# GpSimd takes the last state of a scan unit, its sums stand behind that state, ScalarE's scan copies move behind a product's copy, and the last stores use two queues

## The chip, the cores and the metric

The kernel runs on one core of a Trainium2 chip. The metric is the device time of one execution in microseconds (us); the kernel before is given by the median of three timed runs. A profile of one more execution shows what each engine did: PE (TensorE, the matrix unit; its weight loads are listed as PEld), DVE (VectorE), ACT (ScalarE), POOL (GpSimd) and SP (SyncE, which issues most DMAs). A sequencer's own work is marked with a q behind the engine (SPq, ACTq).

## The reference

Two computations follow each other. The first is a state-space scan (Mamba-2) over 4 batches, 8 heads and 768 time steps with head dimension 32 and state dimension 16:

```python
state = 0
for each chunk c of the sequence:
    cum = cumsum(log(clip(a, 1e-6, 1)))               # within the chunk
    L   = exp(cum[i] - cum[j]) for i >= j, else 0
    y[chunk]  = ((C B^T) * L) x  +  (C state) * exp(cum)
    state     = exp(sum(la)) * state + sum_j exp(cum[-1] - cum[j]) B_j x_j
```

Its output, rearranged to 3072 tokens by 256, goes through a feed-forward block:

```python
h = x @ w_in            # 256 -> 2048
g = h / (1 + exp(-h))   # silu
out = g @ w_out         # 2048 -> 256
```

All inputs and outputs are float32 (the weights arrive as float64 and are rounded on the chip).

## The kernel before, in words

**Units and chunks.** The 3072 tokens are cut into 12 units of 256 tokens, three per batch. Within a unit the scan works on four chunks of 64 tokens, numbered t = 0 to 3. Unit u is the last of its batch when u is 2, 5, 8 or 11, and the first when it is 0, 3, 6 or 9.

**The scan of a unit** is a chain of small functions. `f_P0` and `f_P1` (VectorE) clip the decays and make their running products PFX; `f_E0` and `f_E1` (VectorE) make the products E of the decay matrix; `f_T0` (TensorE) transposes B and C; `f_T1` and `f_T2` (ScalarE) copy the transposes out of PSUM as bh and ce; `f_C` (VectorE) makes cw, C times the running products; `f_B` (GpSimd) makes BT; `f_G` (TensorE) multiplies them; `f_M` (VectorE) applies the decay matrix; `f_D` (ScalarE, four instructions on tile dm) copies each chunk's contribution to the state; `f_S` (VectorE) goes through the chunks and makes the next state from the one before: st[t+1] = st[t] * decay + dm[t], one instruction per chunk (L402), a copy (L400) for the first chunk of a batch. `f_Y` (TensorE) needs st[0] to st[3] of the unit, in this order, and then adds the part within the chunks; `f_X` (ScalarE) copies the result XM out. For a unit that is not the last of its batch, chunk 3 makes the state that the next unit starts from; for a last unit there is no chunk 3 to make, and chunk 2 makes st[3], which the same unit's `f_Y` reads.

**The feed-forward block** runs plainly for units 0 to 3 (`f_s1`, the first layer, eight steps per unit; `s2_list`, the second layer of units 0 and 1). From unit 4 on, units go in pairs G = 2 to 5, and each layer is done by Strassen's scheme in Winograd's form: seven products in place of eight, with sums of blocks before and after them. `f_x1(G, j)` is step j = 0 to 7 of a pair's first layer. Its products are called W, 1, 5, 6, 7, 4, 3, and a string per step (`ORDER`) gives their order; each "s" in the string runs one matrix product of the second layer of the pair before (`s2_pair`, whose seven products run over eight steps each and whose results ScalarE copies out at L549 into ps; GpSimd adds them up at L513). Within a step VectorE adds two products (L628, into gT), and ScalarE copies products (L639, into p or u) and applies silu (L631).

**The sums of the second layer** (`f_TS`, L510) are block differences of gT, 128 x 512 each, all on GpSimd until the last pair: i = 0 and i = 2 (written TN<-gT and gT<-gT) for quarters q = 0 to 3 are issued in the steps 4, 5 and 7 of the pair that makes gT; i = 1 and i = 3 (four each) in steps 1 and 2 of the next pair. The differences of the first layer's input (`f_XT`, L608, tile raw) are GpSimd's too; before pair 2 they are issued in step 7 of unit 3's first layer, ahead of all the sums of pair 1. `f_SO` (L496, eight VectorE instructions of 128 x 512) makes the weights' block sums of the second layer, behind unit 5's states.

**The order on each engine** is the order in which this Python text issues instructions. `scan_plan(G)` gives, for each step of pair G, a list of VectorE (and GpSimd) pieces, a list of ScalarE pieces and a list of TensorE pieces of the scan of pair G + 1: its first unit is scanned in steps 0 to 3, its second in steps 3 to 6. `f_x1` puts the VectorE pieces in at fixed places (`other(dve, 3)` at product 6, `other(dve, 2)` at product 4, one more at the end) and the ScalarE pieces at product 6 (`other(act, 3)`). The scans of units 4 and 5 run beside unit 3's first layer (`scan_piece`). Each engine takes its instructions strictly in this order; a semaphore wait holds back all that stands behind it.

**The end.** The last product "3" is added and stored in two halves of 128 columns (`f_out`): each half is transposed by VectorE and stored by four DMAs, the first half's from SyncE's queue and the second half's from ScalarE's.

## Time and profile before

| | |
|---|---|
| time, median of 3 runs | 381.67 us (379.8 to 382.77) |
| the profiled execution's own time | 382.85 us |
| its span, first to last instruction | 381.1 us |
| PE busy | 356.2 us (93%) |
| DVE, ACT, POOL busy | 197.1, 165.2, 163.4 us |
| granted TensorE clock | 0.994 |

How to read it. The engine that carries the time is TensorE; the question for each stage is where it stands still and whose result it stands still for. The page gives busy times and groups; the answers of the trace give the waits of an engine (total, times, longest), the instructions in order of time (start, duration, engine, line, operation, tiles, count, and in brackets the idle time before it and what ended that), and busy times in chosen stretches. A row of the timeline that ends in x6 is six instructions run together; float32 matmuls are two instructions each here, so "x2" is one product of 128 x 256.

### The profile page before, as it was taken

What the parts mean: (1) busy time and instruction counts of PE and PEld (TensorE: products, weight loads), DVE (VectorE), ACT (ScalarE), POOL (GpSimd) and SP (SyncE); (2) the same over time, 40 slices, a digit from 0 to 9 for tenths busy, and PEclk for the clock granted to TensorE, in tenths of its full rate; (3) what the DMA queues carried; (4) which work ended last, traced back from release to release, by engine and by line L of the source; (5) the groups of instructions that cost most, each with busy time, mean ns of one, the idle gap of its engine ahead of it and who ended that gap; (6) DMA issues with size and microseconds to landing.
All of it is one profiled execution on the core that took longest, in us unless ns stands there. A gap on an engine that the chain in (4) does not pass through costs nothing.

```text
span 381.1 us, 8265 instructions
## 1 busy us (share of the span) xinstructions
PE 356.2 (93%) x3322; PEld 294.2 (77%) x3322; DVE 197.1 (52%) x399; ACT 165.2 (43%) x424; POOL 163.4 (43%) x158
## 2 busy tenths in 40 slices
PE   7876989999999898999998989998999999999994
PEld 3555868888888677778877868886878888888883
DVE  7980998742347766643556623476643322223822
ACT  3652866322322344644453454554445544554010
POOL 2330245233054986075547065638064575281300
PEclk9998999999999999999999999999999999999999
DMA  9997868672843134170136070110010010000202
GB/s 139 186 273 132 311 170 130 75 107 41 128 77 46 41 64 48 28 114 2 28 65 75 12 117 14 25 19 0 2 16 2 15 29 1 15 2 14 33 10 41
DMA packets 124594, 25.20 MB, mean 66 GB/s; under 512 B 118412, under 2 KB 120460, under 8 KB 124556
## 3 DMA queue, kind: packets, MB, share of 16 engines
q1 hardware_dynamic: 121764, 24.35, 35.6%
q10 hardware_dynamic: 2792, 0.33, 0.7%
q8 instruction: 26, 0.43, 0.5%
q14 instruction: 12, 0.10, 0.1%
HBM read 21.52 MB, written 3.15 MB: 65 GB/s over the span
## 4 chain that ended last, share of the span: by engine, by line
PE 74%; DVE 10%; ACT 5%; DMA 4%; issue 3%; SPq 3%; POOL 0%; DVEq 0%; ACTq 0%
PE o_ps L542 22%; PE hp L625 21%; PE hp L451 14%; PE o_ps L465 8%; PE hp L542 3%; PE gy L431 2%; DVE st L402 2%; DVE gT L628 2%; DMA raw<-in_moe_w_in_dram 2%; DVE E L265 2%; PE gy L422 2%; PE gy L365 1%; DVE pb L248 1%; PE gy L310 1%; DMA pa<-in_a_dram 1%
## 5 line engine op out<-in xcount | busy, mean ns | idle before, releaser
L628 DVE TENSOR_TENSOR gT<-hp,p 128x256 f32<-128x256 f32 x64 | 27.1, 423 | 88.9 <-ACT p L639 51.4
L631 ACT ACTIVATE gT<-gT 128x256 f32<-128x256 f32 x96 | 39.7, 414 | 58.1 <-DVE gT L628 58.1
L451 PE MATMUL hp<-XM,w_in_sb 128*128 128x256 f32 x256 | 61.1, 388 | 4.1 <-POOL w_in_sb L167 2.1
L451 PEld LDWEIGHTS hp<-XM,w_in_sb 128*128 128x128 f32 x256 | 49.0, 194 | 12.0 <-POOL w_in_sb L167 4.2
L542 PE MATMUL o_ps<-gT,w_out_sb 128*128 128x256 f32 x224 | 56.8, 380 | 0.4
L513 POOL TENSOR_TENSOR ps<-ps 128x256 f32<-128x256 f32 x28 | 20.3, 725 | 84.2 <-ACT ps L549 76.3
L625 PE MATMUL hp<-raw 128*128 128x256 f32 x192 | 53.1, 381 | 0.0
L542 PEld LDWEIGHTS o_ps<-gT,w_out_sb 128*128 128x128 f32 x224 | 42.2, 190 | 7.3 <-ACT ps L549 1.6
L510 POOL TENSOR_TENSOR gT<-gT 128x512 f32<-128x512 f32 x36 | 46.1, 1294 | 1.6
L625 PEld LDWEIGHTS hp<-raw 128*128 128x128 f32 x192 | 36.0, 190 | 6.1 <-POOL ps L513 0.6
L453 ACT ACTIVATE gT<-hp 128x512 f32<-128x512 f32 x32 | 19.2, 599 | 42.6 <-PE hp L451 42.6
L639 ACT ACTIVATE p<-hp 128x256 f32<-128x256 f32 x64 | 24.7, 385 | 25.8 <-PE hp L625 24.8
L625 PE MATMUL hp<-XM,w_in_sb 128*128 128x256 f32 x128 | 34.1, 389 | 0.0
L628 DVE TENSOR_TENSOR gT<-hp,u 128x256 f32<-128x256 f32 x32 | 13.5, 422 | 33.7 <-PE hp L625 33.1
L465 PE MATMUL o_ps<-w_out_sb,gT 128*128 128x256 f32 x128 | 30.9, 384 | 0.0
L265 DVE TENSOR_TENSOR_SCAN E<-ab,diag 128x256 f32<-128x256 f32 (+1 forms) x32 | 27.4, 883 | 3.6 <-PE gy L431 3.0
L510 POOL TENSOR_TENSOR TN<-gT 128x512 f32<-128x512 f32 x20 | 25.9, 1296 | 6.8 <-ACT gT L631 6.8
L465 PEld LDWEIGHTS o_ps<-w_out_sb,gT 128*128 128x128 f32 x128 | 23.5, 190 | 3.8 <-issue 0.5
L625 PEld LDWEIGHTS hp<-XM,w_in_sb 128*128 128x128 f32 x128 | 22.9, 190 | 4.0 <-issue 1.0
L167 POOL TENSOR_TENSOR w_in_sb<-wu,wv 128x512 uint32<-128x512 uint32 (+1 forms) x9 | 10.6, 1179 | 35.5 <-DVE wv L163 35.5
L302 POOL TENSOR_TENSOR BT<-bct,E 128x256 f32<-128x256 f32 x9 | 5.8, 640 | 44.5 <-issue 14.6
L402 DVE SCALAR_TENSOR_TENSOR st<-st,pfx,dm 128x64 f32<-128x64 f32 x40 | 21.3, 533 | 4.3 <-ACT dm L386 2.7
(114 smaller groups left out, 566.1 us busy)
## 6 DMA issues: line engine op xcount, KB each, us to landing
ab<-in_a_dram SPq DMA_DIRECT2D x40, 128.0 KB, 4.2
raw<-in_moe_w_in_dram SPq DMA_DIRECT2D x8, 512.0 KB, 7.4
raw<-in_moe_w_out_dram SPq DMA_DIRECT2D x8, 512.0 KB, 7.4
xt<-in_x_dram SPq DMA_DIRECT2D x24, 128.0 KB, 3.7
out_dram<-ot SPq DMA_DIRECT2D x76, 32.0 KB, 1.7
bct<-in_C_dram SPq DMA_DIRECT2D x24, 64.0 KB, 3.9
pa<-in_a_dram SPq DMA_DIRECT2D x11, 128.0 KB
bct<-in_B_dram SPq DMA_DIRECT2D x22, 64.0 KB, 4.3
```

Source lines behind the costliest of these rows:

```text
L265: nc.vector.tensor_tensor_scan(out=E[u].rearrange("p k h t -> p (k h t)")[:, Q * g0:Q * (g0 + n)], data0=t.rearrange("p g t -> p (g t)"), ...
L402: nc.vector.scalar_tensor_tensor(out=o, in0=ST[u][:, t], scalar=PFX[u][:, Q * t + Q - 1:Q * t + Q], in1=DM[u][:, k, c], op0=ALU.mult, op1= ...
L451: nc.tensor.matmul(out=hp[:, i], lhsT=w_in_sb[:, kc, f * 128:(f + 1) * 128], rhs=xm[:, kc], start=(kc == 0), stop=(kc == KC - 1))
L453: nc.scalar.activation(GTS[g][:, 2 * j:2 * j + 2], hp, AF.Silu)
L465: nc.tensor.matmul(out=o[:, c], lhsT=GTS[g][:, f, 128 * c:128 * c + 128], rhs=w_out_sb[:, f, :], start=(f == 0), stop=(f == NF - 1), skip_ ...
L510: engine.tensor_tensor(out=o[:, js], in0=a0[:, js], in1=a1[:, js], op=ALU.subtract)
L513: engine.tensor_tensor(out=o, in0=p, in1=q, op=ALU.add)
L542: nc.tensor.matmul(out=o, lhsT=w(j), rhs=g()[:, j], start=(j == 0), stop=(j == NF // 2 - 1))
L625: nc.tensor.matmul(out=o, lhsT=w, rhs=x_, start=start, stop=True, skip_group_check=True)
L628: nc.vector.tensor_tensor(out=o, in0=p, in1=q, op=ALU.add)
L631: nc.scalar.activation(o, i, AF.Silu)
L639: nc.scalar.activation(o, i, AF.Copy)
```

## The change

It has five parts.

1. `f_S`: for units 4 and later, the last state of a unit is made by GpSimd, by two instructions (state times decay, then plus dm) where VectorE used one. Which chunk is the last depends on the unit: 2 for a unit that ends its batch, 3 for others.
2. The second layer's sums i = 0 and i = 2 go through one function `sums`: quarters 0 and 1 in step 4, quarter 2 in step 5 (behind the scan's states in that step's text), and quarter 3 no longer in step 7 but behind step 1 of the next pair. For pair 1 the same applies inside unit 3's first layer, where all of them were in step 7 behind `f_XT`.
3. ScalarE's pieces of the scan (bh, ce, dm, XM) are issued when both product 5 and product 6 have been, so in the steps that do 6 well before 5 they come later: in steps 4 and 5.
4. VectorE's pieces: two (three in steps 1 and 4) at product 6, two at product 4, the rest at the end; `f_C` ahead of the last two `f_E1`; an empty placeholder is gone.
5. The last two halves of the output: each half's four stores alternate between SyncE's queue and ScalarE's.

```diff
@@ f_S
+                p = PFX[u][:, Q * t + Q - 1:Q * t + Q]
+                if u >= 2 * UPB - 2 and t == (2 if last else 3):
+                    nc.gpsimd.tensor_tensor(out=o, in0=ST[u][:, t], in1=p.to_broadcast([128, 64]), op=ALU.mult)
+                    nc.gpsimd.tensor_tensor(out=o, in0=o, in1=DM[u][:, k, c], op=ALU.add)
+                else:
+                    nc.vector.scalar_tensor_tensor(out=o, in0=ST[u][:, t], scalar=p,
+                                                   in1=DM[u][:, k, c], op0=ALU.mult, op1=ALU.add)
@@ f_out
-            (queue or nc.sync).dma_start(
+            (queues or (nc.sync,))[q % len(queues or (0,))].dma_start(
@@ s2_pair, product "3" of the last pair
-                            f_out(P, 0, 1, p["3"], (nc.sync, nc.scalar)[k], (128 * k, 128 * k + 128))
+                            f_out(P, 0, 1, p["3"], (nc.sync, nc.scalar), (128 * k, 128 * k + 128))
@@ f_x1
-        done = ""
+        done, first = "", 3 if j in (1, 4) else 2
...
-                other(dve, 3)
-                other(act, 3)
+                other(dve, first)
...
-        other(dve, 1)
-        other(act, 9)
+            if what in "56" and "5" in done and "6" in done:
+                other(act, 9)
+        other(dve, 9)
@@ scan_plan
-            plan[j + 1][0].extend([E1[2], E1[3], partial(f_C, u), partial(f_B, u, nc.gpsimd)])
+            plan[j + 1][0].extend([partial(f_C, u), E1[2], E1[3], partial(f_B, u, nc.gpsimd)])
-            plan[j + 2][0].extend([partial(f_M, u, 0), partial(f_M, u, 1), lambda: None, partial(f_S, u, 0, 2),
+            plan[j + 2][0].extend([partial(f_M, u, 0), partial(f_M, u, 1), partial(f_S, u, 0, 2),
@@ main
+    def sums(P, j):
+        for q in {4: (0, 1), 5: (2,), 8: (3,)}.get(j, ()):
+            f_TS(P, 0, q, nc.gpsimd)
+            f_TS(P, 2, q, nc.gpsimd)
     for j in range(8):
         f_s1(3, j)
...
-            for q in range(4):
-                f_TS(1, 0, q, nc.gpsimd)
-                f_TS(1, 2, q, nc.gpsimd)
+        sums(1, j)
@@ loop over pairs G
+            if j == 1:
+                sums(G - 1, 8)
...
-            for q in {4: (0, 1), 5: (2,), 7: (3,)}.get(j, ()):
-                f_TS(G, 0, q, nc.gpsimd)
-                f_TS(G, 2, q, nc.gpsimd)
+            sums(G, j)
```

TensorE's order of instructions is the same in both kernels. GpSimd's changes in three places. The first is around unit 5, beside unit 3's first layer; raw<-w_in_sb is the last sum of the first layer's weights, raw<-XM the differences of the pair's input, st the state. Before:

```order
L597 TENSOR_TENSOR raw<-w_in_sb,raw 128x1024
L608 TENSOR_TENSOR raw<-XM 128x256
L608 TENSOR_TENSOR raw<-XM,raw 128x256
L608 TENSOR_TENSOR raw<-XM 128x256
L608 TENSOR_TENSOR raw<-XM,raw 128x256
L510 TENSOR_TENSOR TN<-gT 128x512
L510 TENSOR_TENSOR gT<-gT 128x2x256
L510 TENSOR_TENSOR TN<-gT 128x512
L510 TENSOR_TENSOR gT<-gT 128x2x256
```

After, from the same place on:

```order
L603 TENSOR_TENSOR raw<-w_in_sb,raw 128x1024
L516 TENSOR_TENSOR TN<-gT 128x512
L516 TENSOR_TENSOR gT<-gT 128x2x256
L516 TENSOR_TENSOR TN<-gT 128x512
L516 TENSOR_TENSOR gT<-gT 128x2x256
L405 TENSOR_TENSOR st<-st,pfx 128x64
L406 TENSOR_TENSOR st<-st,dm 128x64
L516 TENSOR_TENSOR TN<-gT 128x512
L516 TENSOR_TENSOR gT<-gT 128x2x256
L614 TENSOR_TENSOR raw<-XM 128x256
```

Four sums now stand between the weights' sum and unit 5's last state, and two more between that state and the input's differences, which were first before.

The second place is GpSimd in steps 1 and 2 of pair 2, where BT is unit 6's, the sums are pair 1's, and ps is an output sum. Before:

```order
L302 TENSOR_TENSOR BT<-bct,E 128x256
L510 TENSOR_TENSOR gT<-gT,TN 128x2x256 x4
L513 TENSOR_TENSOR ps<-ps 128x256
L510 TENSOR_TENSOR gT<-gT 128x2x256 x4
L513 TENSOR_TENSOR ps<-ps 128x256
```

After:

```order
L302 TENSOR_TENSOR BT<-bct,E 128x256
L516 TENSOR_TENSOR TN<-gT 128x512
L516 TENSOR_TENSOR gT<-gT 128x2x256
L516 TENSOR_TENSOR gT<-gT,TN 128x2x256 x4
L519 TENSOR_TENSOR ps<-ps 128x256
L405 TENSOR_TENSOR st<-st,pfx 128x64
L406 TENSOR_TENSOR st<-st,dm 128x64
L516 TENSOR_TENSOR gT<-gT 128x2x256 x4
L519 TENSOR_TENSOR ps<-ps 128x256
```

The last quarter's two sums have come in behind BT, and the state's two instructions stand ahead of the four sums i = 3, which so wait for VectorE's states.

The third place is ScalarE in step 4 of pair 2; p and u are the copies of products, bh and ce the scan's copies of unit 7, ps the copy of a finished product of the second layer. Before:

```order
L639 ACTIVATE u_1772<-hp 128x256
L631 ACTIVATE gT<-gT 128x256
L316 ACTIVATE bh<-gy 128x256
L322 ACTIVATE ce<-gy,par 128x256 x2
L549 ACTIVATE ps<-o_ps 128x2x2x64
L639 ACTIVATE p_1790<-hp 128x256
```

After:

```order
L645 ACTIVATE u_1775<-hp 128x256
L637 ACTIVATE gT<-gT 128x256
L555 ACTIVATE ps<-o_ps 128x2x2x64
L645 ACTIVATE p_1788<-hp 128x256
L316 ACTIVATE bh<-gy 128x256
L322 ACTIVATE ce<-gy,par 128x256 x2
```

The copy of the finished product and the copy of product 5 now come ahead of the scan's three copies; in step 5 dm moves in the same way.

More of the change, by code (lines that the diff above doesn't have):

```diff
@@ L513, in p_add, with f_out @@
         engine.tensor_tensor(out=o, in0=p, in1=q, op=ALU.add)
-    def f_out(P, i, v, c, queue=None, cols=None):
+    def f_out(P, i, v, c, queues=None, cols=None):
         b, t0 = at(2 * P + v)
@@ L834 @@
     P = NU // 2 - 1
+    sums(P, 8)
     S2.append(s2_pair(P, True))
```

2 lines of the change are left out of this document (removed).

## The prediction, made before the changed kernel was run

> **What bounds the kernel now.** The page first.
>
> ```profile
> span 381.1 us, 8265 instructions
> PE 356.2 (93%) x3322; PEld 294.2 (77%) x3322; DVE 197.1 (52%) x399; ACT 165.2 (43%) x424; POOL 163.4 (43%) x158
> ```
>
> TensorE is busy 93% of the span, every other engine about half or less. Its instructions and their order stay as they are, so the change can only move its standstills. Busy times pair by pair say how much there is:
>
> ```profile
> 124.40:185.58 61.18, 56.99 (x546) 46.58 (x545) 33.15 (x63) 27.91 (x80) 37.78 (x37) 1.00 0.31 48
> 185.58:244.32 58.74, 56.21 (x537) 46.66 (x536) 29.90 (x65) 28.10 (x80) 28.97 (x30) 1.00 0.33 51
> 244.32:303.20 58.88, 56.49 (x546) 46.95 (x545) 29.91 (x65) 28.27 (x80) 29.17 (x30) 1.00 0.06 10
> 303.20:351.43 48.23, 48.23 (x224) 42.08 (x224) 11.59 (x28) 23.54 (x63) 24.82 (x24) 1.00 0.08 12
> ```
>
> The first two numbers after the stretch are its length and PE's busy time. Pair 5, without a scan, has no gap: 48.23 us for 112 products, so 0.431 for one and 0.216 for each of its two instructions. Pairs 2 to 4 stand idle for 4.19, 2.53 and 2.39. PE's waits name the releasers:
>
> ```profile
> PE gy L422 <- DVE st L402: 3.7, 6, 0.9
> PE o_ps L542 <- ACT ps L549: 2.5, 3, 0.8
> PE hp L625 <- DVE gT L628: 2.3, 3, 1.7
> ```
>
> Each of the three is one place that comes back in pairs 2, 3 and 4: the states in step 2, a ScalarE copy in step 4, a VectorE sum in step 0. PE's timeline there, and unit 5's `f_Y` (117.71 to 119.12) as an undisturbed measure:
>
> ```profile
> 117.71 0.69 PE L422 MATMUL gy<-cw,st 32*64 32x64 f32 x32
> 119.12 1.99 PE L465 MATMUL o_ps<-w_out_sb,gT 128*128 128x256 f32 x8
> ...
> 128.29 1.46 PE L542 MATMUL o_ps<-gT,w_out_sb 128*128 128x256 f32 x6
> 131.49 0.67 PE L625 MATMUL hp<-raw,w_in_sb 128*128 128x256 f32 x2 [1.74 <-DVE gT L628]
> ...
> 205.96 0.46 PE L422 MATMUL gy<-cw,st 32*64 32x64 f32 x16
> 209.04 1.13 PE L625 MATMUL hp<-XM,w_in_sb 128*128 128x256 f32 x4
> ...
> 218.65 1.03 PE L625 MATMUL hp<-raw 128*128 128x256 f32 x4
> 220.49 1.56 PE L542 MATMUL o_ps<-gT,wu 128*128 128x256 f32 x6 [0.82 <-ACT ps L549]
> ```
>
> From start to start: step 0 of pair 2 loses 131.49 - 128.29 - 6 x 0.216 = 1.90; `f_Y` takes 209.04 - 205.96 = 3.08 where unit 5's took 1.41, so 1.67 lost; step 4 loses 220.49 - 218.65 - 4 x 0.216 = 0.98. A stop costs some 0.16 over the idle time in brackets.
>
> Why VectorE is late stands in its rows beside GpSimd's:
>
> ```profile
> 102.68 1.33 DVE L402 SCALAR_TENSOR_TENSOR st<-st,pfx,dm 128x64 f32<-128x64 f32 x4 [0.67 <-ACT dm L386]
> 126.60 1.20 DVE L248 COPY pb<-pa 128x4 f32<-128x4 f32 x1
> 152.53 0.17 DVE L248 COPY pb<-pa 128x4 f32<-128x4 f32 x1
> 204.25 3.67 DVE L402 SCALAR_TENSOR_TENSOR st<-st,pfx,dm 128x64 f32<-128x64 f32 x3
> ...
> 202.90 4.94 POOL L510 TENSOR_TENSOR gT<-gT 128x512 f32<-128x512 f32 x4
> ```
>
> A state costs 0.33 alone and 1.22 while GpSimd's sums run, about one sum (4.94 / 4 = 1.24); a copy of 128x4 costs 0.17 or 1.20. So each such VectorE instruction waits for the sum in hand. In pair 2's step 0 pair 1's sums run, in step 2 the sums i = 3.
>
> **The change part by part.**
>
> *Step 0.* GpSimd no longer has sums there: quarter 3 waits behind BT in step 1, the others are done earlier. Without the contention the copy falls from 1.20 to 0.17, and one `f_E0` fewer stands before the sum L628. Removed: 1.90 in pair 2; in pairs 3 and 4 (2.3 - 1.74) / 2 = 0.28 idle, 0.45 with the stop's cost. Pair 2 is 2.44 longer than pair 3 at nearly equal work, 1.45 of it by this; of the remaining 1.0 (the same contention in step 1) I take half. Sum -3.3.
>
> *The states in step 2.* They no longer meet the sums i = 3, which now stand behind GpSimd's state. GpSimd's own state isn't in the trace of before. The nearest rows, with those that unit 5 needs below:
>
> ```profile
> 111.58 2.36 POOL L597 TENSOR_TENSOR raw<-w_in_sb,raw 128x1024 f32<-128x1024 f32 x1
> 119.90 3.11 POOL L608 TENSOR_TENSOR raw<-XM 128x256 f32<-128x256 f32 x1 [5.95 <-ACT XM L440]
> 123.09 0.73 POOL L608 TENSOR_TENSOR raw<-XM,raw 128x256 f32<-128x256 f32 x1
> 125.14 1.27 POOL L510 TENSOR_TENSOR TN<-gT 128x512 f32<-128x512 f32 x1
> 195.82 0.64 POOL L302 TENSOR_TENSOR BT<-bct,E 128x256 f32<-128x256 f32 x1 [6.41 <-PE o_ps L542]
> ...
> 117.01 0.60 DVE L402 SCALAR_TENSOR_TENSOR st<-st,pfx,dm 128x64 f32<-128x64 f32 x2 [0.46 <-ACT dm L386]
> 117.53 0.68 DVE L496 TENSOR_TENSOR wu<-w_out_sb 128x512 f32<-128x512 f32 x1
> 121.75 0.69 DVE L496 TENSOR_TENSOR raw<-w_out_sb,wv 128x512 f32<-128x512 f32 x1
> ```
>
> 256 columns more cost 1.27 - 0.73 = 0.54, so 64 columns cost 0.73 - 0.40 = 0.33; at most 0.64, as BT. I take 0.33, the line through the two rows: with a gap, 0.74 for both instructions (1.4 at most). In pair 3 GpSimd starts BT at 195.82, as E ends; then come two sums, four sums and the ps addition: 195.8 + 0.6 + 6 x 1.27 + 0.7 = 204.8. VectorE's states start at 204.25 now, 203.8 with step 0's gain, so two of them may still meet the last sum and the addition; the second is done at 204.9, GpSimd's at some 205.7. PE comes to `f_Y` at 205.96 - 0.4 and asks for the fourth chunk 0.5 later, at 206.1: no wait left, not even in unit 8, where that chunk is GpSimd's. Removed: three times 1.6, -4.8.
>
> *ScalarE's order.* In step 4 the ps copy and product 5's copy come before bh and ce; PE's wait of 0.98 goes, three times, -2.9. bh and ce now come behind two copies more. Between product 5 and their reader `f_G` TensorE still has six products of that step (7, three of the second layer, 4 and 3), 6 x 0.431 = 2.6: covered; without that cover the two copies would cost what bh and ce cost now, about the 0.82 of PE's wait, in each pair. In step 5 dm moves too, and GpSimd's three additions come ahead of the second unit's state; I count 0, since the copy before it and dm itself only change places; bounds -0.98 each, what the same move gives in step 4, and +0.73, unit 11's state behind one addition more. VectorE's other moves (cw ahead of two scans, `f_E0` behind a sum) count 0: VectorE is busy 29.90 of 58.74 there; without that cover a sum would be 0.4 late.
>
> *Unit 5.* Here the change adds a wait. GpSimd ends the weights' sums at 111.58 + 2.36 = 113.94, then has four sums (to about 119.1) ahead of the state that unit 5, a last unit, needs at 117.71 + 0.5 = 118.2. VectorE's two states (the second at 117.01 now) meet the sums and end at about 118.2; behind them stand eight instructions L496, independent of each other, 0.60 apart ((121.75 - 117.53) / 7). The row at 119.90 tells what happens to GpSimd then: work of 0.73 took 3.11, to 123.01, and it ended 0.57 after the last L496 (122.44), although four others had ended since it began. So VectorE's run holds GpSimd off as a whole. From 118.2 the eight take 4.9 and GpSimd's remaining sum 1.27, in whichever order: 124.3; the state 0.7 more: 125.0. PE waits 6.7. All behind it shifts by as much; the six instructions on GpSimd behind the state (two sums, four L608) end by 130.2, before PE, 6.7 later, asks for them. Bounds: 1.9 (119.1, then the state) and 7.0. I take 6.7, for that row is the same pair of instructions.
>
> [...]
>
> *The end.*
>
> ```profile
> 376.47 1.74 SPq L522 DMA_DIRECT2D out_dram<-ot  x4
> 376.83 0.31 DVE L520 STREAM_TRANSPOSE ot<-ps 128x128 f32<-128x128 f32 x1 [0.21 <-DVE ps L566]
> 377.17 1.85 ACTq L522 DMA_DIRECT2D out_dram<-ot  x4
> ```
>
> The last store is issued at 379.02, the eighth of eight. With two of the second half on each queue, both are done two stores after 377.3: 378.2. -0.8; bounds 0 (the landing decides) and -1.0.
>
> *The sum.* -3.3 - 4.8 - 2.9 + 6.7 - 0.8 = -5.1 on the profiled execution, whose time is 382.85 at a span of 381.1: 377.75. That execution lies 1.2 above the median; I put the difference on the median: 381.67 - 5.1 = 376.6. Step 5 at its lower bound in two pairs gives 374.6; the end at 0, step 5 at its upper bound in two pairs give 378.9: the likeliest case's own range, 374.6 to 378.9.
>
> **The rivals.**
>
> *GpSimd gets its turn at unit 5.* For: when single VectorE instructions meet sums (1.22 each), both alternate. Against: the row at 119.90. Without any L496 between, the wait is 1.9, as above. With a turn each from 118.2 on, it is an L496, the sum, an L496, the multiplication, an L496, the addition: 0.60 + 1.27 + 0.60 + 0.33 + 0.60 + 0.33 = 3.7, with a gap 3.8. Without unit 5 the forecast is 369.9, so 371.8 to 373.7. [...]
>
> *The held sums run into the fourth step.* The sums i = 3 start about 3 later than now, and end about where VectorE starts the second unit's running products.
>
> ```profile
> 211.62 0.69 DVE L254 TENSOR_TENSOR_SCAN pfx<-pa,pb 128x256 f32<-128x256 f32 x1
> 213.66 0.42 DVE L628 TENSOR_TENSOR gT<-hp,p 128x256 f32<-128x256 f32 x1 [0.89 <-PE hp L625]
> ```
>
> The scan L254 now ends at 212.31, 1.35 before product 7's sum L628. With PE 2.0 earlier (0.45 and 1.6) L628 is wanted at 211.6; the held sums end at 205.7 + 4.9 = 210.6 in unit 8 and the scan then at some 211.5, just in time. If GpSimd's queue is two sums (2.5) later than I walked it, the states meet sums again (4.8 not gained), and L628 comes 2.3 late in three pairs (6.9): 376.6 + 11.7 = 388.3, slower than before. It decides at 5.1 / 3 = 1.7 of lateness per pair; below 0.1 it costs nothing. Against: no GpSimd row in steps 1 and 2 is longer than its work.
>
> *ScalarE's order only moves the wait.* dm behind product 5's copy makes the second unit's states, then `f_Y`, late by what step 4 gained: 376.6 + 2.9 = 379.5. For: `f_Y` and the states are level there. Against: the states begin about when they do now.
>
> **How the numbers follow.** The forecast 0.60, GpSimd's turn 0.22, the moved wait 0.12, the fourth step 0.06. The predicted time is the forecast's, 376.6. The range goes from 372 (most of the first rival) to 380 (the third rival and the forecast's upper end). One per cent, about what a measurement of this kernel can tell from no change, is 3.8, that is 377.9 and 385.5. Of the forecast's 0.60 some four fifths lie under 377.9: faster 0.48 + 0.22 = 0.70; same 0.12 + 0.12 = 0.24; slower 0.06.
>
> **What would show it.** Right: PE's waits for st and gT in pairs 2 to 4 and for ps in step 4 all but gone; the state copies of 128x4 at 0.17 in step 0; one new wait of PE for GpSimd's st of some 6.7 in unit 5, ahead of pair 2, while L496 runs through; the last ACTq store some 0.8 nearer to the last product. Wrong: a wait for st under 4 there (first rival), waits of PE for gT in step 3 with L248 at 1.2 beside L510 (second), waits of L422 in step 5 (third).

## The result, and the profile after

The changed kernel takes 370.37 us (median of 4, 370.0 to 370.71), the kernel before 381.99 (median of 4, 379.8 to 382.77): a ratio of 0.9705, with a 95% interval of 0.9662 to 0.9747. It is faster, as forecast, but by 11.6 us, where 5.1 were predicted, and the time lies below the range of 372 to 380. One execution among all that were timed, the profiled one of b_tail below, had a mean granted clock of 0.56 and took 605 us; no comparison uses it.

The page of the kernel after, and TensorE's waits in its trace:

```profile
span 368.3 us, 8273 instructions
PE 353.7 (96%) x3320; PEld 294.9 (80%) x3322; DVE 189.2 (51%) x391; ACT 166.0 (45%) x424; POOL 168.1 (46%) x174
...
PE gy L428 <- POOL st L406: 1.6, 2, 1.1
...
PE gy L428 <- DVE st L408: 0.8, 1, 0.8
```

(From the state's line in `f_S` on, a line's number is 6 higher than before: L428 is the line that was L422, L408 was L402, L631 was L625, L634 was L628, L548 was L542, L555 was L549, L471 was L465, L502 was L496, L516 was L510, L614 was L608. L405 and L406 are the two new instructions on GpSimd.) The waits for gT in step 0 and for ps in step 4 are gone from the list, and so are all six for VectorE's st in pairs 2 to 4. Three waits for st are new: one for VectorE's and one of 1.1 for GpSimd's in unit 5, and one of 0.4 for GpSimd's in unit 11. The pairs, in the view by windows, with the same first products as cuts as in the table of before:

```profile
124.76:180.18 55.42, 55.42 (x545) 46.85 (x544) 26.57 (x61) 28.50 (x80) 29.64 (x33) 1.00 0.33 53
180.18:235.21 55.03, 54.99 (x537) 46.74 (x536) 26.19 (x63) 28.27 (x80) 30.26 (x34) 1.00 0.35 54
235.21:291.18 55.97, 55.54 (x547) 47.04 (x546) 26.74 (x63) 28.42 (x80) 30.45 (x34) 1.00 0.07 11
291.18:339.36 48.18, 48.18 (x225) 42.05 (x223) 11.69 (x28) 23.57 (x63) 24.81 (x24) 1.00 0.08 12
```

Unit 5 on TensorE, then GpSimd's rows there, then VectorE's:

```profile
114.01 0.46 PE L428 MATMUL gy<-cw,st 32*64 32x64 f32 x16
115.24 0.34 PE L428 MATMUL gy<-cw,st 32*64 32x64 f32 x8 [0.77 <-DVE st L408]
116.72 0.34 PE L428 MATMUL gy<-cw,st 32*64 32x64 f32 x8 [1.14 <-POOL st L406]
...
117.78 3.59 PE L471 MATMUL o_ps<-w_out_sb,gT 128*128 128x256 f32 x8
...
115.27 0.68 POOL L405 TENSOR_TENSOR st<-st,pfx 128x64 f32<-128x64 f32 x1 [0.16 <-DVE st L408]
116.02 0.65 POOL L406 TENSOR_TENSOR st<-st,dm 128x64 f32<-128x64 f32 x1
116.63 1.72 POOL L516 TENSOR_TENSOR TN<-gT 128x512 f32<-128x512 f32 x1
118.43 1.59 POOL L516 TENSOR_TENSOR gT<-gT 128x512 f32<-128x512 f32 x1
...
112.57 2.62 DVE L408 SCALAR_TENSOR_TENSOR st<-st,pfx,dm 128x64 f32<-128x64 f32 x2 [0.67 <-ACT dm L386]
115.11 0.68 DVE L502 TENSOR_TENSOR wu<-w_out_sb 128x512 f32<-128x512 f32 x1
...
117.14 1.76 DVE L502 TENSOR_TENSOR wv<-wv,w_out_sb 128x512 f32<-128x512 f32 x1
118.82 1.75 DVE L502 TENSOR_TENSOR wu<-w_out_sb 128x512 f32<-128x512 f32 x1
```

The reader is to see three things. The state is done at 116.02 + 0.65 = 116.67, though VectorE's run of L502 had begun at 115.11: the two engines alternate, and both take longer for it (up to 1.76 for an L502 instead of 0.68, up to 1.72 for a sum instead of 1.27). TensorE stops twice, 0.96 and 1.33 from start to start; the first stop waits for VectorE's second state, as its two states took 2.62 beside the sums. And its eight products L471 then take 3.59, where the same eight took 1.99 in the profile before (119.12). The granted clock says why, in the view by windows (the number before the DMA share is PEclk):

```profile
118.00:121.00 3.00, 3.00 (x8) 2.35 (x8) 3.00 (x3) 0.49 (x1) 2.92 (x3) 0.50 0.02 5
```

From 118.02 to 121.43 TensorE has half its clock, which costs 3.41 / 2 = 1.7.

The first profile of before has such a stretch too, at its start, where none of the changed instructions runs:

```profile
PE gy L431 <- issue: 2.8, 1, 2.8
...
28.01 0.45 PE L431 MATMUL gy<-E,xt 64*32 64x64 f32 x32
31.27 0.46 PE L431 MATMUL gy<-E,xt 64*32 64x64 f32 x32 [2.81 <-issue]
...
33.00:35.00 2.00, 2.00 (x6) 1.53 (x6) 0.00 (x0) 0.00 (x0) 0.00 (x0) 0.50 0.66 91
```

TensorE stood 2.8 us waiting for nothing that the profile shows, and then ran at half clock from 32.04 to 35.45. Unit 5's `f_Y` starts at 114.01 after and at 117.71 before. The 3.7 between them arise here: the stop and the half clock make 4.1, and 0.4 go the other way ahead of them (the kernel after is 0.4 later at 25 us).

The tail, ScalarE's last stores after:

```profile
364.40 1.83 ACTq L528 DMA_DIRECT2D out_dram<-ot  x4
```

From the start of the last sixteen products (372.15 before, 360.08 after) to the last store's issue it is 379.02 - 372.15 = 6.87 before and 366.23 - 360.08 = 6.15 after; to the span's end it is 8.97 before and 8.18 after.

Place by place, from one profiled execution to the other (the spans, 381.12 and 368.26, differ by 12.9). The starts of the same matmuls in both traces are subtracted, and a place has the change of this difference from the even stretch ahead of it to the even stretch behind it:

| place | predicted | measured |
|---|---|---|
| start, up to unit 5's `f_Y` | 0 | -3.7 |
| unit 5, to pair 2's first product (6.69 before, 10.75 after) | +6.7 | +4.06, of it 1.7 by half clock |
| pairs 2 to 4, steps 0 and 1 | -3.3 | -2.9, -0.5, -0.5 = -4.0 |
| pairs 2 to 4, `f_Y` in step 2 | -4.8 | -1.8, -1.7, -1.7 = -5.1 (rounded after adding) |
| pairs 2 to 4, step 3 | 0 | +0.3 in pair 2 |
| pairs 2 to 4, step 4 | -2.9 | 3 x -1.1 = -3.3 |
| pairs 2 to 4, step 5 | 0 | 3 x -0.4; its `f_Y` +0.2, -0.1, +0.65: in all -0.4 |
| behind pair 5, to the span's end | -0.8 | -0.8 |

The +0.3 in step 3 comes of the held sums (in a_stdve below the copy takes 0.17 there, and the 0.3 is gone). VectorE's rows there, after:

```profile
149.01 1.12 DVE L248 COPY pb<-pa 128x4 f32<-128x4 f32 x1
...
150.91 0.40 DVE L634 TENSOR_TENSOR gT<-hp,p 128x256 f32<-128x256 f32 x1
```

The four sums i = 3 (L516) now run from 145.09 to 150.10, so the copy of 128x4 meets them and takes 1.12, and the sum L634 starts only when the scan behind the copy is done. The same copy takes 1.12 in step 3 of pairs 3 and 4 too, where TensorE loses nothing: L634 still waits 0.16 for TensorE in pair 3, and not at all in pair 4.

### The profile page after: what moved, and what is told of

It reads as the page before. It is cut to its first block, busy times and chain, and to the rows that moved or that the text cites. A ratio compares the mean times of both kernels' runs of the same rounds, so it can differ in the third digit from the quotient of the medians.

```text
span 368.3 us, 8273 instructions
## 1 busy us (share of the span) xinstructions
PE 353.7 (96%) x3320; PEld 294.9 (80%) x3322; DVE 189.2 (51%) x391; ACT 166.0 (45%) x424; POOL 168.1 (46%) x174
## 4 chain that ended last, share of the span: by engine, by line
PE 85%; DVE 5%; POOL 4%; issue 2%; ACT 2%; DMA 0%; SPq 0%; DVEq 0%; ACTq 0%; POOLq 0%
PE o_ps L548 29%; PE hp L631 26%; PE hp L457 12%; PE o_ps L471 6%; PE hp L548 3%; PE gy L437 2%; PE gy L365 2%; PE gy L428 2%; POOL raw L603 1%; DVE E L265 1%; PE gy L310 1%; PE gy L350 1%; DVE wv L163 1%; PE o_ps L202 1%; PE hp L273 1%
## 5 line engine op out<-in xcount | busy, mean ns | idle before, releaser
L634 DVE TENSOR_TENSOR gT<-hp,p 128x256 f32<-128x256 f32 x64 | 26.9, 421 | 85.2 <-PE hp L631 43.5
L457 PE MATMUL hp<-XM,w_in_sb 128*128 128x256 f32 x256 | 59.8, 382 | 4.0 <-POOL w_in_sb L167 2.5
L548 PE MATMUL o_ps<-gT,w_out_sb 128*128 128x256 f32 x224 | 56.5, 379 | 0.0
L631 PE MATMUL hp<-raw 128*128 128x256 f32 x192 | 52.7, 380 | 0.0
L548 PEld LDWEIGHTS o_ps<-gT,w_out_sb 128*128 128x128 f32 x224 | 42.5, 190 | 5.9
L516 POOL TENSOR_TENSOR gT<-gT 128x512 f32<-128x512 f32 x36 | 46.0, 1293 | 1.6
L631 PEld LDWEIGHTS hp<-raw 128*128 128x128 f32 x192 | 36.2, 190 | 5.4 <-POOL ps L519 0.6
L631 PE MATMUL hp<-XM,w_in_sb 128*128 128x256 f32 x128 | 34.1, 389 | 0.0
L471 PE MATMUL o_ps<-w_out_sb,gT 128*128 128x256 f32 x128 | 32.5, 399 | 0.0
L634 DVE TENSOR_TENSOR gT<-hp,u 128x256 f32<-128x256 f32 x32 | 13.6, 423 | 36.5 <-PE hp L631 34.5
L471 PEld LDWEIGHTS o_ps<-w_out_sb,gT 128*128 128x128 f32 x128 | 24.4, 197 | 4.2 <-issue 0.5
L516 POOL TENSOR_TENSOR TN<-gT 128x512 f32<-128x512 f32 x20 | 25.8, 1292 | 2.3 <-ACT gT L637 2.0
L265 DVE TENSOR_TENSOR_SCAN E<-ab,diag 128x256 f32<-128x256 f32 (+1 forms) x32 | 24.5, 805 | 3.3 <-PE gy L437 3.0
L631 PEld LDWEIGHTS hp<-XM,w_in_sb 128*128 128x128 f32 x128 | 22.9, 190 | 4.0 <-issue 1.0
L555 ACT ACTIVATE ps<-o_ps 128x256 f32<-128x256 f32 x31 | 11.9, 384 | 18.7 <-PE o_ps L548 18.2
```

Of the source, the lines that this page charges most:

```text
L265: nc.vector.tensor_tensor_scan(out=E[u].rearrange("p k h t -> p (k h t)")[:, Q * g0:Q * (g0 + n)], data0=t.rearrange("p g t -> p (g t)"), ...
L457: nc.tensor.matmul(out=hp[:, i], lhsT=w_in_sb[:, kc, f * 128:(f + 1) * 128], rhs=xm[:, kc], start=(kc == 0), stop=(kc == KC - 1))
L471: nc.tensor.matmul(out=o[:, c], lhsT=GTS[g][:, f, 128 * c:128 * c + 128], rhs=w_out_sb[:, f, :], start=(f == 0), stop=(f == NF - 1), skip_ ...
L516: engine.tensor_tensor(out=o[:, js], in0=a0[:, js], in1=a1[:, js], op=ALU.subtract)
L548: nc.tensor.matmul(out=o, lhsT=w(j), rhs=g()[:, j], start=(j == 0), stop=(j == NF // 2 - 1))
L555: nc.scalar.activation(pn, on, AF.Copy)
```

## The experiments

Two theories on unit 5 stood against each other: "hold" (the prediction's: VectorE's run holds GpSimd off as a whole) and "turn" (the first rival's: one instruction of each engine in turn). Beside them: what each part of the change is worth by itself, what half clock follows, and whether the 2.8 at the start belong to the kernel. All kernels below are the kernel after with the edit shown, except where another is named; none leaves work out.

### b_tail: the last stores alone, on the kernel before

```
... (f_out takes several queues, as in the change)
-f_out(P, 0, 1, p["3"], (nc.sync, nc.scalar)[k], (128 * k, 128 * k + 128))
+f_out(P, 0, 1, p["3"], (nc.sync, nc.scalar), (128 * k, 128 * k + 128))
```

> The kernel before with one part of the change alone: the last two output halves' stores alternate between SP's and ScalarE's queue. Two questions. The tail: from TensorE's last product to the end of the span was 381.1 - 375.4 = 5.7 us before and 368.3 - 363.3 = 5.0 us after; the prediction's -0.8 holds if it is 4.9 to 5.0 here, and the landing decides if it is 5.7. The start: in the profile of before TensorE stood 2.8 us at 28.3 us and ran at half clock from 32.0 to 35.4, 3.7 us that the profile of after doesn't have. Theory A: that stop is part of this program; then it is here too, and unit 5's f_Y starts near 117.7. Theory B: it comes in some executions only; then f_Y may start near 114.0 here. By A the time is 381.2, by B between 377.5 and 381.2.

380.52 us (median), ratio to before 0.9958, interval 0.992 to 0.9996: -0.8 in the medians, as predicted, though the interval allows anything from 0.2 to 3. The median lies between what A and B gave. Its profile (see the result) settles nothing about the start; that is left to the profiles of before below.

### a_u5late: GpSimd idle when the state comes

```
-        for q in {4: (0, 1), 5: (2,), 8: (3,)}.get(j, ()):
+        for q in ({5: (0, 1, 2), 8: (3,)} if P == 1 else {4: (0, 1), 5: (2,), 8: (3,)}).get(j, ()):
```

> The kernel after, but pair 1's sums of quarters 0 and 1 are issued behind unit 5's states, together with quarter 2's, and not ahead of them. GpSimd is then idle when VectorE has done its two states (about 113.2 us), and its own state arrives in the run of eight L502. Theory 'hold' (the prediction's): the run of about 4.9 us ends first, the state is done at about 118.8, TensorE waits 4.3 us where it now waits 2.3, and the time is 2 or more above the kernel after. [...]

372.24 us (371.92 to 372.94; ratio 0.9769, 0.9719 to 0.9818). GpSimd's rows, the start of VectorE's run, and TensorE's first wait behind them:

```profile
113.55 0.29 POOL L405 TENSOR_TENSOR st<-st,pfx 128x64 f32<-128x64 f32 x1 [3.36 <-DVE st L408]
113.92 0.65 POOL L406 TENSOR_TENSOR st<-st,dm 128x64 f32<-128x64 f32 x1
...
124.56 1.17 POOL L614 TENSOR_TENSOR raw<-XM 128x256 f32<-128x256 f32 x1
...
113.59 0.80 DVE L502 TENSOR_TENSOR wu<-w_out_sb 128x512 f32<-128x512 f32 x1
...
125.79 0.76 PE L631 MATMUL hp<-raw 128*128 128x256 f32 x2 [3.79 <-POOL raw L614]
```

The state is done at 114.57, 0.98 after the run on VectorE began: "hold" is out for this place. TensorE doesn't stop in `f_Y`. But the six sums, each lengthened to 1.6 or 1.7 beside an L502, put `f_XT` off to 124.56, and TensorE waits 3.8 for it. Behind that the matmul at 126.34 takes 0.64, where the one at 120.75 took 0.38, and the execution's mean granted clock is 0.993. The wait was moved, not removed; that `f_XT` might come late behind the six sums stands in the expectation of a_u5both, below. The time comes near the one that "hold" gave, for another reason, which only the trace tells.

### a_u5dve and a_u5both: unit 5's last state by VectorE

```
-                if u >= 2 * UPB - 2 and t == (2 if last else 3):
+                if u >= 2 * UPB and t == (2 if last else 3):
```

> The kernel after, but unit 5's last state is VectorE's, as before the change. Its third state then meets the sum that GpSimd has in hand until 115.1 us and ends at about 115.4; TensorE's last chunk of f_Y starts at 115.5, not 116.7: 1.2 us less. Theory 'half clock comes of the length of the stop': without the second stop the clock stays full, another 1.6 less, 367.6 in all. Theory 'the first stop is enough': 369.2. The prediction's own reading (GpSimd held off by L502) would give 6.7 less than a kernel that waits 6.7, which the kernel after doesn't.

367.01 us (366.72 to 367.42; ratio 0.963, 0.9582 to 0.9678), 3.4 less than the kernel after. One stop is left in unit 5:

```profile
PE gy L428 <- DVE st L408: 0.9, 1, 0.9
```

The execution's mean granted clock is 0.997, where one stretch of 3.41 us at half clock would by itself make 0.995 (1.7 of 365): there is no such stretch behind this stop. So the theory on the length of the stop fits: 1.2 of stop and the clock's share go together, 367.6 expected. In all four executions the mean clock is 0.997 or more; still, a stop this short had half clock behind it in b_again, below. a_u5both has both edits:

> The kernel after, with unit 5's last state by VectorE and pair 1's sums behind it. No state meets a sum, so no wait for st in unit 5 by any theory and no half clock behind it: 370.4 - 2.3 - 1.6 = 366.5, if f_XT, which then stands behind six sums on GpSimd, is still done before pair 2's first step asks for it; if it isn't, the wait moves there (six sums of 1.27 end at about 121 to 125 beside L502, f_XT four additions of 0.73 later, TensorE at about 121).

368.18 us (367.57 to 368.36; ratio 0.9661, 0.9604 to 0.9718). The expectation was wrong in one point: with the state on VectorE nothing on GpSimd waits any more, so the sums "behind the states" run as early as before and meet the states as in a_u5dve (the same single wait of 0.9). The kernel is a_u5dve in unit 5; between the two traces 0.8 had arisen ahead of it, in the first 30 us.

### a_actold: ScalarE's order undone

```
                 other(dve, first)
+                other(act, 3)
...
-            if what in "56" and "5" in done and "6" in done:
-                other(act, 9)
         other(dve, 9)
+        other(act, 9)
```

> The kernel after with one part undone: ScalarE's scan copies stand again where they stood before the change (bh and ce behind the copy of product 6, the rest at the step's end). The prediction put -2.9 on this part: 370.4 + 2.9 = 373.3, with TensorE's wait for the ps copy in step 4 back at 0.98 in each of pairs 2 to 4. The two traces also show 0.4 in step 5 in each of pairs 2 to 4, which the prediction counted as 0; if it comes of the same part, 373.3 + 0.6 = 373.9 (0.55 came back in unit 11). The rival 'it only moves the wait' gives 370.4.

372.67 us (371.09 to 373.84; ratio 0.9765, 0.9691 to 0.9838): +2.3 in the medians, +2.6 by the last product in the traces. The wait is back, though smaller:

```profile
PE o_ps L548 <- ACT ps L555: 1.0, 3, 0.3
```

By the starts of the same matmuls, step 4 loses 0.6 and step 5 loses 0.4 in each pair, and 0.2 come back in unit 7's `f_Y`: 2.7 in all. So the part alone is worth nearly what was predicted (2.9), but some 1.2 of it stand in step 5, which had been counted as 0, and of step 4's 3.3 it brings back only 1.8. The rest, by the rows, is VectorE's order. In the kernel before ScalarE's bh waited for VectorE's cw, in each of pairs 2 to 4; in a_actold, where `f_C` still stands ahead of the last two scans, it doesn't wait. Before, then a_actold:

```profile
160.31 0.38 ACT L316 ACTIVATE bh<-gy 128x256 f32<-128x256 f32 x1 [0.39 <-DVE cw L333]
...
155.55 0.38 ACT L316 ACTIVATE bh<-gy 128x256 f32<-128x256 f32 x1
```

The rival "it only moves the wait" is out.

### a_sumold, a_stdve, a_bothold: the sums' places and the state on GpSimd

```
# a_sumold
-        for q in {4: (0, 1), 5: (2,), 8: (3,)}.get(j, ()):
+        for q in ({7: (0, 1, 2, 3)} if P == 1 else {4: (0, 1), 5: (2,), 7: (3,)}).get(j, ()):
# a_stdve
-                if u >= 2 * UPB - 2 and t == (2 if last else 3):
+                if False:
# a_bothold: both
```

> The kernel after with one part undone: pair 1's sums stand again behind f_XT in unit 3's last step, and the later pairs' quarter 3 in the pair's last step. The prediction put -3.3 on it in step 0; the two traces show 2.7 in pair 2, 0.3 in pair 3 and 0.6 in pair 4. In unit 5 GpSimd is idle when its state comes, as in the run in which the sums stand behind the states: TensorE's wait and the half clock behind it, 3.65 in all, should be gone. So 370.4 + 3.6 - 3.65 = 370.3. A second question: in the profile of before the first f_XT came in the middle of the run of eight on VectorE, from an idle GpSimd, and took 3.11, while since then every GpSimd instruction that was there before the run began alternated with it. Theory M: who arrives in the middle of a run is held to its end; then the first f_XT takes about 3 here too (it is released some 2 us after the run's start). Theory T: always a turn each; then it takes at most 1.2.

369.3 us (368.65 to 369.89; ratio 0.9678, 0.9623 to 0.9734). Unit 5 gains 4.0, pair 2's steps 0 and 1 give 2.8 back and its step 3 gains the 0.3; pairs 3 and 4 lose nothing. Theory M is out:

```profile
117.08 1.04 POOL L614 TENSOR_TENSOR raw<-XM 128x256 f32<-128x256 f32 x1 [1.90 <-ACT XM L446]
...
116.86 0.68 DVE L502 TENSOR_TENSOR wu<-w_out_sb 128x512 f32<-128x512 f32 x1
117.46 1.21 DVE L502 TENSOR_TENSOR wv<-w_out_sb 128x512 f32<-128x512 f32 x1
```

`f_XT` comes in the middle of the run and gets its turn ahead of the L502 that starts at 117.46.

> The kernel after with one part undone: every state is VectorE's again. Unit 5 alone is 3.3 faster so (367.0). In step 2 of pairs 2 to 4 the sums i = 3 no longer stand behind GpSimd's state. Theory of the prediction: they then run as soon as GpSimd is free, the states meet them at 1.2 each as before, and TensorE's 1.6 comes back three times: 367.0 + 4.8 = 371.8. Theory 'the held quarter 3 is enough' (two sums more stand ahead of the sums i = 3): the states stay at 0.3 and the time is 367.0.

368.17 us (367.9 to 368.47; ratio 0.9649, 0.9595 to 0.9704). TensorE's waits for VectorE's st:

```profile
PE gy L428 <- DVE st L408: 1.8, 2, 0.9
```

One of the two is unit 5's, the other unit 6's: only in pair 2 does the old wait come back (1.3 from start to start), in pairs 3 and 4 it doesn't (under 0.2). The second theory is right for two pairs of three.

> The kernel after with two parts undone together: the states are VectorE's again, and the sums stand where they stood before. Undone alone, the places of the sums left the states of step 2 alone, and the states cost 1.15 in pair 2 and nothing in pairs 3 and 4. Theory A: in pairs 3 and 4 either part is enough by itself, and only both together bring the old 1.7 back: then unit 5 is 3.65 faster than in the kernel after, pair 2's first step 2.5 slower, step 2 slower by 1.8 + 1.7 + 1.7: 370.4 - 3.65 + 2.5 + 5.2 = 374.5; with the 0.3 and 0.6 that the first steps of pairs 3 and 4 gained and that no part undone alone brought back, 375.4. Theory B: pairs 3 and 4 gained by ScalarE's and VectorE's order; then step 2 there stays as in the kernel after: 371.0.

373.84 us (371.64 to 376.91; ratio 0.9816, 0.974 to 0.9893), and in its trace

```profile
PE gy L428 <- DVE st L408: 3.1, 5, 0.9
PE hp L631 <- DVE gT L634: 1.5, 2, 1.3
```

`f_Y` in step 2 loses 0.9, 1.7 and 1.7 against the kernel after: theory A, though the four executions spread over 5 us. In pairs 3 and 4 either part alone takes the states out of the sums' way, and only both undone bring the wait back.

The 0.5 that steps 0 and 1 of pairs 3 and 4 gained each came back in no variant. The rows of pair 3 suggest that two parts give it there too, either by itself. In a_sumold the copy of 128x4 meets a sum again, but with VectorE's new order L634 comes right behind the scan; in a_dveold (next) one L283 stands ahead of L634 again, but the copy is short, and L634 still waits for TensorE:

```profile
182.20 1.19 DVE L248 COPY pb<-pa 128x4 f32<-128x4 f32 x1
184.16 0.40 DVE L634 TENSOR_TENSOR gT<-hp,p 128x256 f32<-128x256 f32 x1
...
182.12 0.17 DVE L248 COPY pb<-pa 128x4 f32<-128x4 f32 x1
184.12 0.42 DVE L634 TENSOR_TENSOR gT<-hp,p 128x256 f32<-128x256 f32 x1 [0.52 <-PE hp L631]
```

No run undid the sums' places and VectorE's order together, so this is read from the rows and not shown.

### a_dveold: VectorE's order undone

```
-        done, first = "", 3 if j in (1, 4) else 2
+        done = ""
-                other(dve, first)
+                other(dve, 3)
...
-        other(dve, 9)
+        other(dve, 1)
-            plan[j + 1][0].extend([partial(f_C, u), E1[2], E1[3], partial(f_B, u, nc.gpsimd)])
+            plan[j + 1][0].extend([E1[2], E1[3], partial(f_C, u), partial(f_B, u, nc.gpsimd)])
... (and the empty piece ahead of f_S)
```

> The kernel after with one part undone: VectorE's scan pieces stand in the old order (three behind product 6, f_C behind the last two f_E1, the empty piece ahead of the states). The prediction counted this part as 0: 370.4, with no wait of TensorE in pairs 2 to 4 that the kernel after doesn't have. The other reading: part of the 0.3 to 0.7 that the first step of each pair gained, beyond the copies of 128x4, is a sum of VectorE (0.4) that comes earlier; then up to 0.4 in each pair comes back: 371.6.

370.11 us (368.95 to 373.16; ratio 0.9712, 0.9643 to 0.9782), and the last product 0.1 later than in the kernel after. Nothing, as predicted, but only beside the other parts: with ScalarE's old order VectorE's new one is worth some 0.5 in step 4 of each pair (a_actold).

### b_again and b_again2: the kernel before, two profiles more

> The kernel before once more, for another profile. 24 times of it so far fall into two groups, 379.0 to 381.7 and 382.3 to 383.8, and its first profile is of the upper one (382.85). Theory: the groups differ by TensorE's stop at 28.3 us and the half clock behind it (3.7 in the first profile). Then a profile with a time in the lower group shows no stop over 1 us there, code that is loaded at about 26 us instead of 28.6, and unit 5's f_Y at 114 to 115; one in the upper group shows the stop again. Also open: whether the first f_XT addition takes 3.1 beside the run of eight again.

> The kernel before a third time, for a profile, with the same two readings as the second: a time in the lower group and no stop, or a time in the upper group and the stop at 28.3 us.

380.75 and 380.69. Neither has the stop: TensorE waits 0 and 0.4 there, and `f_Y` of unit 5 starts at 113.9 and 113.8. The load of instructions (a packet of 16 KB in the queue of that kind) that starts at 28.56 in the first profile starts ahead of 28.4 in b_again and at 26.3 in the kernel after. So the 3.7 at the start were an event of that one execution. But b_again has a half clock elsewhere, in pair 2 at step 2's stops (0.45 and 0.88 in the first profile):

```profile
146.00:147.00 1.00, 1.00 (x59) 0.83 (x37) 0.05 (x1) 0.42 (x1) 0.00 (x0) 0.59 0.00 0
147.00:148.00 1.00, 1.00 (x3) 0.82 (x3) 0.00 (x0) 0.00 (x0) 0.00 (x0) 0.50 0.00 0
148.00:149.00 1.00, 1.00 (x3) 0.74 (x3) 0.00 (x0) 0.18 (x1) 0.00 (x0) 0.50 0.00 0
149.00:150.00 1.00, 1.00 (x5) 0.85 (x4) 0.73 (x3) 0.21 (x1) 0.00 (x0) 0.70 0.00 0
```

By the mean clocks of these windows it lasts from 146.2 to 149.6, which costs 3.4 / 2 = 1.7. In b_again2 the mean granted clock is 0.992, in b_again 0.995; where b_again2's was low isn't shown here. The times go with the clock. 27 executions of the kernel before, timed beside the experiments, have a mean granted clock beside their time:

| mean granted clock | executions | time, median (lowest to highest) |
|---|---|---|
| 0.999 or 1.0 | 6 | 379.4 (379.0 to 380.7) |
| 0.993 to 0.997 | 9 | 380.6 (379.7 to 381.4) |
| 0.984 to 0.989 | 12 | 383.2 (382.8 to 383.8) |

(The mean counts the half clock behind the last product too, 0.50 from 380.20 on in the first profile, which costs nothing. One stretch of 3.41 alone makes 0.9955, so 0.996 and 0.997 need not hold one.) The expectation that the upper group is the group with the stop falls: the profile that has the stop lies at a clock of 0.994, and the upper group's missing clock, 0.012 x 381 = 4.6 us, is that of more than one such stretch. No profile of that group was taken.

### d_shift1 and d_shift3: the moment at which GpSimd arrives

In the first profile of before and in a_bothold the first `f_XT` takes 3.11; in after, a_u5late and a_sumold it takes 1.04 to 1.17. The two kernels are a_bothold with one and three small VectorE instructions (zeros into a tile that nothing reads any more) ahead of the run of eight.

```
+        if j == 6:
+            for _ in range(1):          # 3 in d_shift3
+                nc.vector.memset(hm[:, 0:4], 0.0)
         if j >= 6:
             f_SO(2 * j - 12)
```

> The kernel with both the states and the sums as before (a_bothold), and one memset of 128x4 on VectorE (0.06 us and a gap, as L249) ahead of its run of eight in unit 3's step 6. In a_bothold the first f_XT came to GpSimd at 115.78, 0.04 before the start of VectorE's next L502, and was held 3.1 to the run's end; in the kernel with only the sums' places undone it came 0.38 before the next start and was held 0.3. Theory 'moment of arrival': with the run 0.1 to 0.2 later, f_XT comes 0.13 to 0.25 ahead of the next start and is held under 1. Theory 'how the run began' (without GpSimd in it, the run holds it off whenever it comes): about 3 again, less the shift.

> The same with three memsets: the run starts 0.3 to 0.4 later, f_XT comes 0.3 to 0.45 ahead of the next start, as in the kernel in which it was held 0.3. Theory 'moment of arrival': 1.0 to 1.2 for the first f_XT. Theory 'how the run began': 2.7 to 2.9.

a_bothold, GpSimd's row and VectorE's row ahead of which it comes:

```profile
115.78 3.11 POOL L614 TENSOR_TENSOR raw<-XM 128x256 f32<-128x256 f32 x1 [5.95 <-ACT XM L446]
...
115.81 0.68 DVE L502 TENSOR_TENSOR wu<-w_out_sb 128x512 f32<-128x512 f32 x1
```

d_shift1, the same two:

```profile
116.38 0.73 POOL L614 TENSOR_TENSOR raw<-XM 128x256 f32<-128x256 f32 x1 [5.96 <-ACT XM L446]
...
116.43 1.23 DVE L502 TENSOR_TENSOR wu<-w_out_sb 128x512 f32<-128x512 f32 x1
```

The shift came out smaller than expected, some 0.02 by the rows: in a_bothold GpSimd's instruction stands 0.03 ahead of VectorE's next start, in d_shift1 0.05 ahead. That is enough: it takes 0.73 there, VectorE's takes 1.23, and the next two alternate with them, at 117.19 (1.05) and 117.58 (1.21). In d_shift3 it comes 0.31 ahead and takes 0.99:

```profile
116.43 0.99 POOL L614 TENSOR_TENSOR raw<-XM 128x256 f32<-128x256 f32 x1 [5.96 <-ACT XM L446]
...
116.74 1.22 DVE L502 TENSOR_TENSOR wu<-w_out_sb 128x512 f32<-128x512 f32 x1
```

In these runs "moment of arrival" holds, and "how the run began" is out. The held ones came 0.03 (a_bothold) and 0.04 (before) ahead; those that came from an idle GpSimd into a running run and weren't held came 0.05 (d_shift1, one execution), 0.31 (d_shift3) and 0.38 (a_sumold) ahead. (At the first L502 of a run, 0.04 ahead wasn't held in a_u5late.) Why one that comes too late for one start then misses the three after it too, no run shows. The two took 372.56 and 372.85 in their one execution.

### c_best: a version that may beat both

```
-        for q in {4: (0, 1), 5: (2,), 8: (3,)}.get(j, ()):
+        for q in ({4: (0,), 5: (1,), 7: (2,), 8: (3,)} if P == 1 else {4: (0, 1), 5: (2,), 8: (3,)}).get(j, ()):
```

> A version that may beat both: the kernel after, but of pair 1's sums only quarter 0's stand ahead of GpSimd's state in unit 5, quarter 1's behind it, quarter 2's behind f_XT. VectorE's states then meet no sum, GpSimd's state follows at once, f_XT stands behind two sums and not six, and two sums fall into pair 2's first step and not eight. Expected: no wait for st in unit 5 and no half clock (3.65 less than the kernel after), f_XT in time, and 0 to 0.8 back in pair 2's first step: 366.8 to 367.5. If f_XT is late or the first step loses more, it is no better than the version with unit 5's state on VectorE alone (367.0).

366.97 us (366.55 to 367.67; ratio 0.9612, 0.9562 to 0.9661). Unit 5 doesn't stop; in pair 2's first step 0.75 came back, one wait of TensorE:

```profile
PE hp L631 <- DVE gT L634: 0.5, 1, 0.5
```

It beats both kernels, by 3.4 the one after, and is level with a_u5dve, which needs one constant changed. Against the kernel after, two sums of pair 1 have moved behind GpSimd's state, and two behind `f_XT`.

## Why the prediction was right and where it failed

The direction and the places were right. *Step 0* (-3.3; -4.0 measured), *the states in step 2* (-4.8; -5.1), *ScalarE's order* in step 4 (-2.9; -3.3) and *the end* (-0.8; -0.8) came out within 0.7 each. In step 0 the 0.7 are mostly the half of step 1's 1.0 in pair 2 that the prediction left out: nearly all of it came. Three reasons behind these terms were too narrow. The states in pairs 3 and 4 are freed by the sums' new place or by GpSimd's state, either one. Of what ScalarE's order gives by itself, 1.2 is in step 5, which the prediction put at 0 with bounds of -0.98 and +0.73. And step 4 also gained from VectorE's `f_C`, which had been counted as 0; that 2.7 for the part alone lies so near to 2.9 is partly luck. The loss in unit 11 that those bounds named did come, at 0.65.

Three steps failed.

*"So VectorE's run holds GpSimd off as a whole ... I take 6.7, for that row is the same pair of instructions."* This is the mis-sized term: +4.06 measured, 2.3 of it in stops of TensorE. The row at 119.90 is no accident, it returns at 3.11 in a_bothold; but it is the row of an instruction that arrived 0.04 ahead of a start. The one that arrived 0.05 ahead (0.73 in d_shift1), and those that were there as the run began (0.65 to 1.72 in after), alternated. One row was taken for a rule, against the rows of 1.22. Of the 2.3 only 1.33 wait for GpSimd's state. The other 0.96 wait for VectorE's second state: the prediction has VectorE's two states done 0.5 behind the start of `f_Y`, and beside the sums they were done 1.2 behind it. The first rival, at 0.22, had the alternation, and the wait lies within its 1.9 to 3.8; its time, 371.8 to 373.7, was missed for the reason of the third step below. In the places read here the two engines alternate, but in that row GpSimd's instruction stood through four starts of VectorE's (119.94 to 121.75).

*"A stop costs some 0.16 over the idle time in brackets."* In unit 5 they cost 1.7 more: the profile of after has half clock for 3.41 us behind the two stops (the profiled executions of a_actold and a_dveold, with the same waits of 0.8 and 1.1, have a mean clock of 0.995 and 0.993). That 1.7 is in the +4.06. Without it the term would have been mis-sized by 4.3.

*"That execution lies 1.2 above the median; I put the difference on the median."* The sum was made against times that hold events of this kind: in the kernel before, the stops of step 2 (the longest 0.88) are followed by a half clock in pair 2 of b_again and by none in the first profile (1.00 in pairs 2 to 4), and once 3.7 came at the start (the wait "L431 <- issue: 2.8" stood in the view of waits and was left out of the argument). The change takes these stops away, and in the profile of after pairs 2 to 4 have a clock of 1.00. The parts sum to 4.06 - 4.0 - 5.1 + 0.3 - 3.3 - 0.4 - 0.8 = -9.2. From the median of before (381.99) that gives 372.8; from those executions of before that have nearly full clock (379.4) it gives 370.2, and 370.37 was measured. So of the 6.2 by which the forecast missed, 2.6 are unit 5's term, 1.4 the pairs, which gained 12.4 for 11.0, and the rest, some 2.3, is 381.67 - 379.4, what the median of before held beyond the stops themselves. This last share is worked out from the table of clocks, not measured place by place.

The held sums did run into the fourth step, as the second rival had it: L248 takes 1.12 beside L516 in step 3 of all three pairs. It cost 0.3 in pair 2 and nothing in the others, where the rival needed GpSimd 1.7 later to change the result; the prediction's "just in time" was right. The third rival didn't happen: no wait of L428 in step 5 but unit 11's.

## What to carry to other kernels

The price of a stop of TensorE can be more than its length: in unit 5 stops of 2.3 us had another 1.7 of half clock behind them. Look for the granted clock in windows of a microsecond, and when the times of a kernel lie in groups, set its mean granted clock beside them before a sum is made against the median. A row that contradicts the others of its kind (3.11 among rows of 1.2) is to be explained before it carries a term; here a shift of some 0.02 us undid it. And where VectorE and GpSimd hold each other up, the instruction that TensorE waits for should not stand behind or beside the other's long run: moving one state of unit 5 back to VectorE, or putting fewer sums ahead of it, was worth 3.4 us. Where two parts of a change take away the same wait, undoing one of them shows nothing, as for the states of pairs 3 and 4: undo both before a part is called worthless.

## What the runs showed of the hardware

- Half clock came in stretches of some 3.4 us, with 0.50 in the view by windows: 32.04 to 35.45 in before, 118.02 to 121.43 in after, 146.2 to 149.6 in b_again. It set in 0.77 us (before) and 1.30 us (after) behind the stop's end. It followed stops shorter than itself: 0.77 and 1.14 idle within 3 us in unit 5 of after, and step 2's in pair 2 of b_again; in the first profile of before the same place's 0.45 and 0.88, and one stop of 1.74, passed at a clock of 1.00. In the 3.41 us ahead of it TensorE was busy for 0.46 us (before) and 1.64 us (after): what sets it off, no run here shows. Nor is it certain behind unit 5's two stops: one execution of a_actold and one of a_dveold have a mean clock of 0.999 and 0.997, and each is 1.2 to 1.6 us below the median.
- One GpSimd addition of 128x256 was held for a run of four VectorE instructions (3.11 in a_bothold), and another got its turn at once (0.73 in d_shift1); their arrivals differ by some 0.02 us (0.03 against 0.05 ahead of VectorE's next start). Where the two engines alternated in unit 5 of after, an addition of 128x512 took 1.59 to 1.72 on GpSimd instead of 1.27, and up to 1.76 on VectorE from start to end instead of 0.68.
- TensorE stood 2.8 us at its instructions once (before, up to 31.27), where a load of instructions started at 28.56; in after, where it started at 26.3, it didn't. That it was the load that TensorE waited for is argued from the times, not shown.
